# A recurrent cell and a routed layer on one core: the routed layers of the first two batches run one behind the other, with the second batch ranked and gathered in the same step

## Chip, core and metric

The kernel runs on one core of one Trainium2 chip. The metric is the device time of one execution in microseconds (us). Everything is float32, except the one-hot selection of the ranking, which is bfloat16.

## What is computed

An mLSTM cell runs over 4 batches, 8 heads, 768 positions and 40 features per head. Its output, seen as 320 features per position, goes through a "mixture of depths": per batch, the 128 positions with the highest score pass through a two-layer network and are added back.

```python
for t in range(S):                                  # mLSTM, per batch and head
    m_new = maximum(f_gate[t] + m, i_gate[t])
    f_stab, i_stab = exp(f_gate[t] + m - m_new), exp(i_gate[t] - m_new)
    C = f_stab * C + i_stab * outer(v[t], k[t])
    n = f_stab * n + i_stab * k[t]
    y[t] = sigmoid(o_gate[t]) * (C @ q[t]) / maximum(abs(n @ q[t]), 1.0)
x = y as (batch, position, 320)
scores = x @ w_gate                                 # routed layer, per batch
top = the 128 positions with the highest scores
out = x
out[top] = x[top] + sigmoid(scores[top]) * (relu(x[top] @ w1) @ w2)   # w1 320 x 1024, w2 1024 x 320
```

## The kernel before

The order of all instructions is written out by hand: each engine runs its own instructions in the order in which the Python functions issue them, and semaphores make it wait for operands and for buffers. The engines are TensorE (PE, matmuls and transposes), VectorE (DVE), ScalarE (ACT), GpSimd (POOL) and SyncE (SP, which issues the loads).

The cell is cut into 12 steps `n` of 256 positions, three per batch (batch 0 is steps 0 to 2, batch 3 is steps 9 to 11). The loop over `n` (line 658) computes step `n` and prepares step `n + 1`:

- `scores(n)` (L292) multiplies keys and queries on PE; `masked(n)` (L303) applies the causal mask on DVE and so gives the tile `P`.
- `turn(n + 1, "kT")` and `turn(n + 1, "qT")` (L223) transpose keys and queries on PE, and ACT copies them out of the matmul's accumulator memory (PSUM); `widen(n + 1)` (L214) is an ACT copy that the query transposes need.
- `weigh(n + 2)` (L239) multiplies values by gates on POOL; `update(n + 1)` (L259) forms the new state on PE and `states(n + 1)` (L271) adds it up on DVE.
- `read(n)` (L310) and `attend(n)` (L327) accumulate the step's output on PE; `divide(n)` (L336) normalizes it on DVE; `sigmoid(n)` (L247, four ACT instructions) and `output(n)` (L349, two POOL products) apply the output gate; `store(n)` (L357) issues two stores to DRAM from POOL's queue.
- `router(n)` (L364) computes the scores of the routed layer on DVE.

The routed layer of a batch `b` goes through this chain:

- `spread(b)` (L397): six PE transposes spread the 768 scores over all partitions, and ACT copies them out.
- `ranks(b)` (L422): DVE counts for three columns how many scores are greater (L415), ACT does so for the other three by signs (L420); `select(b)` (L467) builds the one-hot selection on DVE.
- `numbers(b)` (L510): six small PE matmuls give the positions, and `index(b)` (L473) turns them into indices with four small DVE instructions.
- `fetch(b)` (L517): POOL issues an indirect DMA that gathers the 128 rows from the stored output in DRAM.
- `fetched(b)` (L524): three PE transposes of the gathered rows, three ACT copies; `valued(b)` (L536): the gate of each row, on DVE and ACT.
- `layer1(b, f0)` (L545): half of the first layer, 12 matmuls and one ACT relu. With `b == 0` it works before the change on both halves of the tiles `xeT_t` and `hT_t`, 256 columns, which are batches 0 and 1 together. `layer2(b)` (L565): 8 matmuls per batch; `weighed(b)` (L575): ACT scales the result out of PSUM; `add(b)` (L584): POOL issues an indirect DMA that adds the rows to the output in DRAM.

PSUM is held by four pools: `ps_s`, `ps_u` and `ps_h` with one buffer each of two banks, and `ps_t` with two buffers of one bank each. Scores, `spread` and the second half of the first layer share `ps_s`; state updates and the first half of the first layer share `ps_u`; `read`/`attend` hold `ps_h` until `divide` has read it; transposes, gathered rows and `layer2` rotate through `ps_t`. So a tile is written only when the reader of its predecessor in that buffer has finished.

The chain of batch 0 stands before the change in steps 3 (`spread`), 4 (`ranks`, `select`, `numbers`) and 5 (`fetch`); that of batch 1 in steps 6 (`spread`) and 7 (`ranks`, `select`, `numbers`, `fetch`). Step 8 is written out in the function `layers` (L625): both batches are transposed there, their first layer runs in two halves over 256 columns, and the sigmoids, outputs, stores and scores of steps 6, 7 and 8, left out in steps 6 and 7, are done between. The third batch is spread, ranked and selected there too, with its numbers and its gather in step 9.

Of the kernel before, what the change touches and what calls it, by code (L numbers as in the profile page):

```python
# [9 lines left out]
FP = mybir.dt.float32  # L10
# [16 lines left out]
def _fast(ctx, tc, q, k, v, i_gate, f_gate, o_gate, w_gate, w1_in, w2_in, out):  # L27
# [6 lines left out]
    NS = S // 256  # L34
# [179 lines left out]
    def widen(n):  # L214

        ACT.copy(out=qw_t[n % 2][:, :, :, 0:D], in_=q_t[n % NB].rearrange("s h (t d) -> s t h d", t=2))  # L216
# [30 lines left out]
    def sigmoid(n):  # L247
        for r in range(2):
            for c in range(2):
                ACT.activation(out=so_t[n % 3][64 * c:64 * c + 64, r], in_=o_t[n % NO][64 * r:64 * r + 64, c], func=AF.Sigmoid)  # L250
# [76 lines left out]
    def attend(n):  # L327
        g = pending[n]
        for p in range(NP):
            for j in range(2):  # L330
                for c in range(2):
                    PE.matmul(g["pH"][64 * c:64 * c + 64, NP * j + p], g["P"][:, j, c, p, :], wv_t[n % 3][:, c, 2 * p + j],  # L332
                              start=(c, j) not in g["begun"], stop=True, skip_group_check=True)
                    g["begun"].add((c, j))

    def divide(n):  # L336
        b, s = divmod(n, NS)
        pH = pending[n]["pH"].rearrange("s h r x -> s r h x")
        den = work.tile([128, 2, H], FP, name="den")
        nq = pH[:, :, :, D]  # L340
        DVE.scalar_tensor_tensor(out=den, in0=nq, scalar=-1.0, in1=cols[s][:, 2:4, b * H:b * H + H], op0=OP.mult, op1=OP.max)
        DVE.scalar_tensor_tensor(out=den, in0=nq, scalar=LEAST * LEAST, in1=den, op0=OP.max, op1=OP.max)
        rec = work.tile([128, 2, H], FP, name="rec")
        DVE.reciprocal(out=rec, in_=den)
        y = work.tile([128, 2, H, D], FP, name="y", bufs=4)
        DVE.tensor_tensor(out=y, in0=pH[:, :, :, 0:D], in1=rec.unsqueeze(3).to_broadcast([128, 2, H, D]), op=OP.mult)
        pending[n]["y"] = y

    def output(n):  # L349
        b, s = divmod(n, NS)  # L350
        for r in range(2):
            x, o = x_t[b % 2][:, 2 * s + r, 0:DM], so_t[n % 3][:, r].rearrange("s h d -> s (h d)")
            order = "s (p j d) -> s j p d"
            POOL.tensor_tensor(out=x.rearrange(order, j=2, d=D), in0=pending[n]["y"][:, r].rearrange("s (j p) d -> s j p d", j=2),  # L354
                               in1=o.rearrange(order, j=2, d=D), op=OP.mult)

    def store(n):  # L357
        b, s = divmod(n, NS)
        for c in range(2):
            a = 256 * s + 128 * c  # L360
            (POOL if n < N - 1 else SP).dma_start(out=out[b, a:a + 128, :].rearrange("(r t) d -> t r d", t=64),  # L361
                          in_=x_t[b % 2][64 * c:64 * c + 64, 2 * s:2 * s + 2, 0:DM])
# [31 lines left out]
    def half(b):  # L394
        return slice(128 * (b % 2), 128 * (b % 2) + 128)
# [128 lines left out]
    def fetched(b, count=0):  # L524
        d, xe = dep[b], xe_t[b % 2]
        pX = ps_t.tile([128, 3, 128], FP, name="pX", tag="t")
        fill(pX[:, 0, :], count)
        for j in range(3):
            w = min(128, DM - 128 * j)
            PE.transpose(pX[0:w, j, :], xe[:, 128 * j:128 * j + w], ident)  # L530
        d["xeT"] = xeT_t[:, :, half(b)]
        ACT.copy(out=d["xeT"][:, 0:2], in_=pX[:, 0:2])
        for i in range(2):
            ACT.copy(out=d["xeT"][64 * i:64 * i + 64, 2], in_=pX[0:64, 2])

    def valued(b):  # L536
        d, xe = dep[b], xe_t[b % 2]
        scr = work.tile([128, DM], FP, name="scr", bufs=1)
        sg = mod.tile([128, 1], FP, name="sg")
        DVE.tensor_tensor_reduce(out=scr, in0=xe[:, 0:DM], in1=wg, scale=1.0, scalar=0.0, op0=OP.mult, op1=OP.add,  # L540
                                 accum_out=sg)
        d["g"] = mod.tile([128, 1], FP, name="g")
        ACT.activation(out=d["g"], in_=sg, func=AF.Sigmoid)

    def layer1(b, f0):  # L545

        d = dep[b]
        w = 256 if b == 0 else 128
        xeT, hT = (xeT_t, hT_t) if b == 0 else (xeT_t[:, :, half(b)], hT_t[:, :, half(b)])
        if b in (0, B - 1) and f0 > 0:  # L550
            ph = ps_s.tile([128, 2, 512], FP, name="ph", tag="s")
        else:
            ph = ps_u.tile([128, 2, 512], FP, name="pU")
        ph = ph[:, :, 0:2 * w].rearrange("s i (f e) -> s f i e", e=w)
        for f in range(4):
            for j in range(2):
                PE.matmul(ph[:, f // 2, f % 2, :], w1[:, j, (f0 + f) * 128:(f0 + f) * 128 + 128], xeT[:, j, :],  # L557
                          start=(f < 2 and j == 0), stop=False, skip_group_check=True)
        for f in range(4):
            o = slice(64 * (f % 2), 64 * (f % 2) + 64)  # L560
            PE.matmul(ph[:, f // 2, f % 2, :], w1c[o, (f0 + f) // 2, :], xeT[o, 2, :], start=False, stop=True,  # L561
                      skip_group_check=True)
        ACT.activation(out=hT[:, f0:f0 + 4, :].rearrange("s (f i) e -> s f i e", i=2), in_=ph, func=AF.Relu)
# [61 lines left out]
    def layers(n):  # L625

        fetched(0)
        read(n)
        fetched(1)
        attend(n)  # L630
        divide(n)
        valued(0)
        valued(1)
        for i in range(n - 2, n + 1):
            sigmoid(i)
            output(i)
            store(i)
            if i < n:
                layer1(0, 4 * (i - n + 2))
            router(i)  # L640
        weigh(n + 1)
        layer2(0)
        dep[2] = {"sb": spread(2, 0, 2 * NS, ps_h)}
        ranks(2)
        weighed(0)
        layer2(1)
        add(0)
        weighed(1)
        select(2)
        weigh(n + 2)  # L650
        turn(n + 1, "kT")
        widen(n + 1)
        update(n + 1)
        states(n + 1)
        turn(n + 1, "qT")
        add(1)

    for n in range(N):
        b, s = divmod(n, NS)
        more = n + 1 < N  # L660
        todo = queue.get(n, ())
        for act, i in zip(todo[0::2], todo[1::2]):
            act(*(() if i is None else (i,)))
        scores(n)
        masked(n)
        if n == 8:
            layers(n)
            continue
        if n == 0:
            update(0)  # L670
            states(0)
        if n in (3, 6, 11):
            router(n - 1)
        if n in (4, 7):
            ranks(n // 3 - 1)
            select(n // 3 - 1)
        if more:
            turn(n + 1, "kT", (0, 2, 6, 2, 2, 4)[n] if n < 6 else 0)
            widen(n + 1)
        if 0 < n and more:  # L680
            update(n + 1)
            if n != 9:
                states(n + 1)
            if n not in (3, 6, 7, 9):
                router(n - 1)
        if not more:
            sigmoid(n)
            gated(n)
            fill(ps_t.tile([128, 128], FP, name="pf", tag="t"), 2)
        read(n)  # L690
        if n == 9:
            numbers(2, ps_s.tile([128, 2, 512], FP, name="pi", tag="s")[:, 0, 0:3])
            states(n + 1)
        if n + 2 < N and n != 7:
            weigh(n + 2)
        if n == 5:
            fetch(0)
        if n == 0:
            update(1)
            states(1)  # L700
        if more:
            turn(n + 1, "qT")
            if n in (3, 6):
                dep[n // 3 - 1] = {"sb": spread(n // 3 - 1, 0, 2 * NS)}
            if n == 7:
                numbers(1, spare(n + 1)[:, 1, 0:3])
                fetch(1)
            if n not in (6, 7):
                sigmoid(n)
        else:  # L710
            fetched(b - 1, 2)
            dep[b] = {"sb4": spread(b, 0, 4)}
            layer1(b - 1, 0)
            valued(b - 1)
            ranks_first(b)
        attend(n)
        divide(n)
        if n == 4:
            numbers(0, spare(n + 1)[:, 1, 0:3])
        if n == 9:  # L720
            fetch(2)
        if more and n not in (6, 7):
            output(n)
            store(n)
        if n == 0:
            POOL.memset(k_t[3][:, :, :, D:DP], 0.0)
            tables()
        if n == 1:
            margins()
# [376 lines left out]
```

## Time and profile before

| what | value |
|---|---|
| time, median of 3 runs | 167.95 us (167.4 to 170.14) |
| the profiled execution: its own time | 168.06 us |
| its span, first to last instruction | 166.2 us |
| granted clock of TensorE, mean (1 is full speed) | 0.952 |
| PE busy | 147.9 us, 89% of the span |
| DVE busy | 94.2 us, 57% |
| ACT busy | 88.6 us, 53% |
| POOL busy | 84.3 us, 51% |
| HBM traffic | 143 GB/s over the span |

How to read the profile: a row of a timeline or of a group gives the start and the length in us, the engine, the line of the kernel, the operation, `out<-in` by tile names, the operands' shapes and how many instructions are merged (`x32`); in square brackets stands how long the engine sat idle before it and what ended that. A float32 matmul of the source shows as two records, so 16 matmuls are `x32`. The rows of the chain of waits give start, length and what it was, each step being what released the next. A row of the windows of one engine gives the stretch, its length, the busy time with the number of instructions, the granted clock, the busy share of the DMA engines and their GB/s. Under DMA, "to landing" is the time from a transfer's issue to its last byte.

### The profile page before, as it was taken

To read this page: it belongs to the slowest core of one execution; us is meant where nothing else is said; L and a number is where in the kernel's file an instruction comes from. 1 tells how busy PE (TensorE), PEld (TensorE's weight loads), DVE (VectorE), ACT (ScalarE), POOL (GpSimd) and SP (SyncE) were. 2 spreads that over 40 slices of the span, in tenths; PEclk is the share of its full clock that TensorE was granted. 3 is DMA by queue.
4 is the path that set the end of the run, shared out by engine and by line. 5 is a ranking of instruction groups with operands and counts; after the bars stand their busy time and mean duration, and the time that the engine had idled before them with its cause. 6 is when DMAs were issued, how large, how long until landed. Compare 5 with 4: busy or idle time off the path is not lost.

```text
span 166.2 us, 6581 instructions
## 1 busy us (share of the span) xinstructions
PE 147.9 (89%) x2816; PEld 127.7 (77%) x2816; DVE 94.2 (57%) x251; ACT 88.6 (53%) x177; POOL 84.3 (51%) x114
## 2 busy tenths in 40 slices
PE   7999899999989899994949999997999999999900
PEld 7889789897978898894838786766899898898600
DVE  6567466477689966898513322465496969511010
ACT  1577397556698545792011566593577859312000
POOL 7146379878582859920200476956775644122020
PEclk9999999999999999999675899999999999999985
DMA  4999899999979999999989999973313030330110
GB/s 89 196 161 191 146 175 204 185 222 183 224 154 237 173 209 187 201 351 185 300 181 172 187 236 238 187 153 43 43 28 93 7 83 0 79 43 6 43 51 2
DMA packets 91880, 24.31 MB, mean 146 GB/s; under 512 B 88097, under 2 KB 90466, under 8 KB 91842
## 3 DMA queue, kind: packets, MB, share of 16 engines
q1 hardware_dynamic: 89920, 18.75, 63.2%
q0 software_dynamic: 1728, 4.92, 11.4%
q8 instruction: 24, 0.39, 1.0%
q10 hardware_dynamic: 194, 0.13, 0.3%
q14 instruction: 14, 0.11, 0.2%
HBM read 19.20 MB, written 4.59 MB: 143 GB/s over the span
## 4 chain that ended last, share of the span: by engine, by line
PE 55%; DMA 12%; DVE 10%; ACT 7%; issue 7%; POOL 4%; SPq 0%; POOLq 0%; DVEq 0%; ACTq 0%
PE pt L232 9%; PE pH L332 7%; PE pU L557 6%; DMA xe<-out_dram,idx 6%; PE pU L267 6%; PE py L573 5%; PE pH L322 3%; PE pS L300 3%; DMA k<-in_k_dram 3%; PE warm L99 3%; DMA v<-in_v_dram 3%; POOL wv L244 2%; ACT sgn L420 2%; PE ph L557 2%; PE pU L561 2%
## 5 line engine op out<-in xcount | busy, mean ns | idle before, releaser
L244 POOL TENSOR_TENSOR wv<-v,cols 64x656 f32<-64x656 f32 x23 | 30.3, 1318 | 21.2 <-DMA v<-in_v_dram 7.5
L354 POOL TENSOR_TENSOR x<-y,so 128x320 f32<-128x320 f32 x24 | 21.4, 904 | 23.7 <-ACT so L250 15.1
L250 ACT ACTIVATE so<-o 64x320 f32<-64x320 f32 x48 | 22.5, 468 | 0.9
L236 ACT COPY qT<-pt 128x512 f32<-128x512 f32 x24 | 13.8, 634 | 16.0 <-PE pt L232 16.0
L369 DVE CUSTOM_DVE_ANT_0 scr<-x,wg 128x320 f32<-128x320 f32 x22 | 13.7, 623 | 14.1 <-POOL x L354 12.9
L234 ACT COPY kT<-pt 128x512 f32<-128x512 f32 x24 | 13.1, 586 | 12.0 <-PE pt L232 12.0
L332 PE MATMUL pH<-wv,P 128*64 128x82 f32 x384 | 18.4, 255 | 0.0
L573 PE MATMUL py<-w,hT 128*128 128x320 f32 x64 | 18.1, 436 | 0.0
L332 PEld LDWEIGHTS pH<-wv,P 128*64 128x64 f32 x384 | 16.3, 150 | 2.0 <-issue 1.6
L267 PE MATMUL pU<-wv,k 128*64 128x82 f32 x384 | 16.5, 237 | 1.0 <-issue 0.6
L267 PEld LDWEIGHTS pU<-wv,k 128*64 128x64 f32 x384 | 14.5, 137 | 3.0 <-issue 2.7
L300 PE MATMUL pS<-qT,kT 40*64 40x64 f32 x768 | 15.0, 226 | 1.6 <-ACT qT L236 1.1
L306 DVE TENSOR_TENSOR P<-pS,mask 128x1024 f32<-128x1024 f32 x12 | 14.6, 1218 | 2.4 <-PE pS L300 2.2
L279 DVE TENSOR_TENSOR C<-pU,C 128x164 f32<-128x164 f32 x40 | 13.1, 327 | 4.9 <-PE pU L267 3.8
L300 PEld LDWEIGHTS pS<-qT,kT 40*64 40x64 f32 x768 | 13.1, 140 | 3.2 <-ACT qT L236 1.5
L573 PEld LDWEIGHTS py<-w,hT 128*128 128x128 f32 x64 | 11.8, 190 | 4.8 <-issue 0.3
L361 POOL DMA_DIRECT2D out_dram<-x x22 | 13.9, 634 | 3.3 <-POOL x L354 3.3
L232 PE MATMUL pt<-ident,k 128*128 128x128 f32 x96 | 13.9, 282 | 0.8 <-DMA k<-in_k_dram 0.6
L322 PE MATMUL pH<-C,qT 40*64 40x41 f32 x704 | 13.7, 229 | 0.0
L232 PE MATMUL pt<-ident,qw 128*128 128x128 f32 x96 | 13.0, 279 | 0.6 <-ACT qw L216 0.5
L322 PEld LDWEIGHTS pH<-C,qT 40*64 40x64 f32 x704 | 12.4, 134 | 1.4 <-issue 0.5
L420 ACT ACTIVATE sgn<-sb,x 128x768 f32<-128x768 f32 (+2 forms) x16 | 12.8, 801 | 0.5
(141 smaller groups left out, 220.6 us busy)
## 6 DMA issues: line engine op xcount, KB each, us to landing
k<-in_k_dram SPq DMA_DIRECT2D x24, 160.0 KB, 4.8
q<-in_q_dram SPq DMA_DIRECT2D x12, 320.0 KB, 5.1
v<-in_v_dram SPq DMA_DIRECT2D x24, 160.0 KB, 4.5
o<-in_o_gate_dram SPq DMA_DIRECT2D x24, 160.0 KB, 4.6
out_dram<-x POOLq DMA_DIRECT2D x22, 160.0 KB, 3.9
w<-in_moe_w_dram SPq DMA_DIRECT2D x2, 640.0 KB
w<-in_moe_w_dram SPq DMA_DIRECT2D x2, 512.0 KB
out_dram<-x SPq DMA_DIRECT2D x2, 160.0 KB
```

The source lines that it names most:

```text
L232: PE.transpose(pt[:, p, :], src[:, c, 2 * p:2 * p + 2, :].rearrange("s j d -> s (j d)"), ident)
L244: (DVE if n == 0 and r else POOL).tensor_tensor(out=wv_t[n % 3][o, :, :, r], in0=v_t[n % NB][o], op=OP.mult, in1=cols[s][o, 0:2, b * H:b * ...
L250: ACT.activation(out=so_t[n % 3][64 * c:64 * c + 64, r], in_=o_t[n % NO][64 * r:64 * r + 64, c], func=AF.Sigmoid)
L267: PE.matmul(pU[64 * j:64 * j + 64, c, p], k_t[n % NB][:, c, 2 * p + j, :], wv_t[n % 3][:, c, 2 * p + j], start=True, stop=True)
L300: PE.matmul(pS[o, j, c, p, :], kT[e, p, t], qT[e, p, t], start=True, stop=True)
L306: DVE.tensor_tensor(out=P.rearrange(flat), in0=pending[n].pop("pS").rearrange(flat), op=OP.mult, in1=mask.unsqueeze(1).to_broadcast([128, ...
L322: PE.matmul(g["pH"][64 * c:64 * c + 64, NP * j + p, r], g["qT"][e, p, t], state[n, 2 * c + r][e, p, :], start=(c, j) not in g["begun"], st ...
L332: PE.matmul(g["pH"][64 * c:64 * c + 64, NP * j + p], g["P"][:, j, c, p, :], wv_t[n % 3][:, c, 2 * p + j], start=(c, j) not in g["begun"], ...
L354: POOL.tensor_tensor(out=x.rearrange(order, j=2, d=D), in0=pending[n]["y"][:, r].rearrange("s (j p) d -> s j p d", j=2), in1=o.rearrange(o ...
L361: (POOL if n < N - 1 else SP).dma_start(out=out[b, a:a + 128, :].rearrange("(r t) d -> t r d", t=64), in_=x_t[b % 2][64 * c:64 * c + 64, 2 ...
L420: ACT.activation(out=sgn[:, 0:w], in_=sb, func=AF.Sign, bias=own, scale=-1.0, accum_out=cnt)
L573: PE.matmul(d["py"], hT_t[:, f, half(b)], w2[:, f, :], start=(f == 0), stop=(f == NF - 1))
```

## The change

In step 8 the first layer of batch 0 runs alone over 128 columns (two halves, with `divide(8)` behind the second on DVE), then its second layer; behind them come the transposes of the gathered rows of batch 1 and its first layer, and later its second layer. Batch 1 is spread in step 7 instead of 6, behind the query transposes, and its `ranks`, `select`, `numbers` and `fetch` move from step 7 into step 8: the counts stand behind the mask of step 8, the numbers between the two halves of batch 0's first layer, and the gather behind the store of step 6 on POOL's queue. The numbers use a `ps_t` buffer there instead of a corner of the state's tile. The second half of the first layer uses `ps_s` for every batch but batch 2. The sigmoids, outputs and stores of steps 6, 7 and 8 keep their order but are spread between the new pieces; the routers of steps 6 and 7 stand behind `layer2(0)`, that of step 8 behind the first half of batch 1's first layer. `add(0)` stands directly behind `weigh(9)`, the key transposes of step 9 ahead of `spread(2)`, and `update(9)` behind `weigh(10)` and `select(2)` as before. The gather of batch 0 is issued in step 6, behind `weigh(8)`, instead of step 5.

```diff
@@ -545,9 +545,9 @@
     def layer1(b, f0):
 
         d = dep[b]
-        w = 256 if b == 0 else 128
-        xeT, hT = (xeT_t, hT_t) if b == 0 else (xeT_t[:, :, half(b)], hT_t[:, :, half(b)])
-        if b in (0, B - 1) and f0 > 0:
+        w = 128
+        xeT, hT = xeT_t[:, :, half(b)], hT_t[:, :, half(b)]
+        if b != 2 and f0 > 0:
             ph = ps_s.tile([128, 2, 512], FP, name="ph", tag="s")
         else:
             ph = ps_u.tile([128, 2, 512], FP, name="pU")
@@ -626,30 +626,43 @@
 
         fetched(0)
         read(n)
-        fetched(1)
+        ranks(1)
+        select(1)
         attend(n)
+        layer1(0, 0)
+        sigmoid(n - 2)
+        output(n - 2)
+        store(n - 2)
+        numbers(1, ps_t.tile([128, 3], FP, name="pi", tag="t"))
+        fetch(1)
+        layer1(0, 4)
         divide(n)
         valued(0)
+        sigmoid(n - 1)
+        output(n - 1)
+        store(n - 1)
+        layer2(0)
+        router(n - 2)
+        router(n - 1)
+        weighed(0)
+        sigmoid(n)
+        output(n)
+        store(n)
+        fetched(1)
         valued(1)
-        for i in range(n - 2, n + 1):
-            sigmoid(i)
-            output(i)
-            store(i)
-            if i < n:
-                layer1(0, 4 * (i - n + 2))
-            router(i)
+        layer1(1, 0)
+        router(n)
+        layer1(1, 4)
         weigh(n + 1)
-        layer2(0)
+        add(0)
+        turn(n + 1, "kT")
+        widen(n + 1)
         dep[2] = {"sb": spread(2, 0, 2 * NS, ps_h)}
         ranks(2)
-        weighed(0)
         layer2(1)
-        add(0)
         weighed(1)
         select(2)
         weigh(n + 2)
-        turn(n + 1, "kT")
-        widen(n + 1)
         update(n + 1)
         states(n + 1)
         turn(n + 1, "qT")
@@ -671,9 +684,9 @@
             states(0)
         if n in (3, 6, 11):
             router(n - 1)
-        if n in (4, 7):
-            ranks(n // 3 - 1)
-            select(n // 3 - 1)
+        if n == 4:
+            ranks(0)
+            select(0)
         if more:
             turn(n + 1, "kT", (0, 2, 6, 2, 2, 4)[n] if n < 6 else 0)
             widen(n + 1)
@@ -693,18 +706,15 @@
             states(n + 1)
         if n + 2 < N and n != 7:
             weigh(n + 2)
-        if n == 5:
+        if n == 6:
             fetch(0)
         if n == 0:
             update(1)
             states(1)
         if more:
             turn(n + 1, "qT")
-            if n in (3, 6):
-                dep[n // 3 - 1] = {"sb": spread(n // 3 - 1, 0, 2 * NS)}
-            if n == 7:
-                numbers(1, spare(n + 1)[:, 1, 0:3])
-                fetch(1)
+            if n in (3, 7):
+                dep[n // 4] = {"sb": spread(n // 4, 0, 2 * NS)}
             if n not in (6, 7):
                 sigmoid(n)
         else:
```

## The prediction

> **What bounds the kernel now.** I read the page first, then the chain of waits, then TensorE's windows and timeline around step 8. Batches are 0 to 3; step 8 is the last of batch 2. Times are us from the span's start.
>
> ```profile
> span 166.2 us, 6581 instructions
> PE 147.9 (89%) x2816; PEld 127.7 (77%) x2816; DVE 94.2 (57%) x251; ACT 88.6 (53%) x177; POOL 84.3 (51%) x114
> ```
>
> TensorE (PE) is busy 89% of the span, so an edit is worth what it gives PE: idle time taken away, or slow time.
>
> ```profile
> 73.22 0.94 DVE cmp L415 x2
> ...
> 76.38 0.96 DVE sel L469
> ...
> 78.36 0.31 PE pU L514 x6
> ...
> 80.03 6.28 DMA xe<-out_dram,idx
> ...
> 89.64 5.02 PE pU L557 x16
> ```
>
> The chain leaves PE in step 7: DVE ranks batch 1 and builds its selection, PE's six numbers matmuls wait for that, the second gather waits for them, and `attend` of step 8 stands behind the gather.
>
> ```profile
> 68.33 0.82 PE L405 MATMUL pB<-ident,x 128*128 128x128 f32 x6
> 69.08 1.36 PE L332 MATMUL pH<-wv,P 128*64 128x82 f32 x32
> ...
> 75.02 1.09 PE L232 MATMUL pt<-ident,qw 128*128 128x128 f32 x8
> 78.36 0.29 PE L514 MATMUL pU<-place,sel 128*128 128x3 bf16 x6 [2.25 <-DVE C L279]
> 78.58 2.37 PE L332 MATMUL pH<-wv,P 128*64 128x82 f32 x32
> 80.88 1.71 PE L300 MATMUL pS<-qT,kT 40*64 40x64 f32 x64
> ...
> 86.35 0.90 PE L530 MATMUL pX<-ident,xe 128*128 128x128 f32 x3 [2.21 <-DMA xe<-out_dram,idx]
> ```
>
> Two holes of 2.25 and 2.21 us. The same 32 matmuls of `attend` take 1.36 in step 6 and 2.37 in step 7; the windows of PE (busy time, then granted clock) say why:
>
> ```profile
> 75.39:78.80 3.41, 1.16 (x17) 0.99 1.00 178
> 78.80:82.21 3.41, 3.41 (x84) 0.51 0.99 272
> 82.21:85.63 3.42, 1.93 (x94) 0.99 1.12 292
> 85.63:89.04 3.41, 2.69 (x31) 0.50 0.69 117
> 89.04:92.45 3.41, 3.41 (x17) 0.51 1.21 194
> ```
>
> After a stretch of 3.41 us with 1.16 or 1.93 us of work the clock stands at half for the next; it stays there after 2.69 of work, and comes back only after a full stretch. So the holes cost 4.5 us of idleness and three stretches at half speed.
>
> **The change part by part.** Durations come from this execution: 166.2 of span and 1.9 around it are its 168.06; the median of the runs is 167.95, so the two are within 0.1%.
>
> *Steps 5 to 7.* The first gather's issue leaves step 5 for step 6, behind `weigh(8)`:
>
> ```profile
> 64.70 1.14 POOL L520 DMA_INDIRECT xe<-out_dram,idx  x1 [0.28 <-POOL wv L244]
> ...
> 69.16 2.66 POOL L244 TENSOR_TENSOR wv<-v,cols 64x656 f32<-64x656 f32 x2
> ...
> DMA to landing us min/median/max: 3.0/3.7/6.3
> ```
>
> On POOL it stood ahead of `output(5)`, so that, its store and `weigh(8)` come 1.1 earlier and the gather itself 6 later, at 70.7 (71.82 less 1.1). By the longest landing seen it is there at 77.0; it is needed at 78.5 (below). I cost it at nothing; uncovered it would cost as much as it is late. `spread(1)` leaves step 6: PE gains 0.75 (68.33 to 69.08), and pays it again in step 7. The three counts, the halving, the selection (4.1 of DVE, 73.22 to 77.34) and the numbers leave step 7, and the 2.25 hole with them. PE ends step 7's transposes at 75.35 (76.11 less 0.75), `spread(1)` at 76.1, `attend(7)` at full clock at 77.4 (before: 80.95), `scores(8)` at 78.5, the first gather's transposes at 78.9.
>
> ```profile
> 80.99 0.17 DVE L341 SCALAR_TENSOR_TENSOR den<-pH,cols 128x16 f32<-128x16 f32 x1 [1.69 <-PE pH L332]
> ...
> 81.69 0.82 DVE L346 TENSOR_TENSOR y<-pH,rec 128x640 f32<-128x640 f32 x1
> 82.66 1.23 DVE L306 TENSOR_TENSOR P<-pS,mask 128x1024 f32<-128x1024 f32 x1
> ```
>
> `divide(7)` takes 1.5 on DVE (80.99 to 82.51), so DVE ends it at 78.9 and masks step 8 by 80.1. `read(8)` fits under the mask; `attend(8)` runs from 80.1 to 81.4.
>
> ```profile
> 95.65 3.72 PE L557 MATMUL ph<-xeT,w 128*128 128x256 f32 x16
> 99.30 1.13 PE L561 MATMUL ph<-xeT,w1c 64*128 64x256 f32 x8
> 100.36 4.58 PE L573 MATMUL py<-w,hT 128*128 128x320 f32 x16
> ...
> 111.15 1.35 PE L267 MATMUL pU<-wv,k 128*64 128x82 f32 x32
> 114.44 1.16 PE L300 MATMUL pS<-qT,kT 40*64 40x64 f32 x64 [0.77 <-ACT qT L236]
> 136.67 2.05 PE L557 MATMUL pU<-xeT,w 128*128 128x128 f32 x16
> 138.65 0.72 PE L561 MATMUL pU<-xeT,w1c 64*128 64x128 f32 x8
> ```
>
> Before, the layers began behind it at 89.6 (the chain's last row): PE is 8.2 us ahead there.
>
> *The layers.* A half of the first layer over both batches takes 4.7 at full clock (95.65 to 100.36); over one batch 2.6 (the last rows, less their overlap). Four of 2.6 against two of 4.7 add 1.0 of PE. After `attend(8)` comes the first of them, to 84.0. DVE counts and selects from 80.1 to 84.3 (4.1 as above), so the numbers wait 0.3 and end at 84.6; the second half ends at 87.2 and `layer2(0)`, 4.5, at 91.7. Here the new wait stands: PE's next work is the second gather's transposes.
>
> ```profile
> 92.30 1.93 ACT L250 ACTIVATE so<-o 64x320 f32<-64x320 f32 x4
> 139.47 0.58 ACT L563 ACTIVATE hT<-pU 128x512 f32<-128x512 f32 x1
> 109.57 0.93 ACT L582 ACTIVATE yg<-py,g 128x320 f32<-128x320 f32 x2
> 87.29 0.37 ACT L532 COPY xeT<-pX 128x256 f32<-128x256 f32 x1 [3.40 <-PE pX L530]
> 93.33 2.10 POOL L354 TENSOR_TENSOR x<-y,so 128x320 f32<-128x320 f32 x2 [12.21 <-ACT so L250]
> 95.73 1.25 POOL L361 DMA_DIRECT2D out_dram<-x  x2 [0.30 <-POOL x L354]
> ...
> DMA to landing us min/median/max: 4.0/4.0/4.1
> ```
>
> POOL issues that gather behind `output(6)` and `store(6)`. From the start of the four sigmoids to the end of the store's issue it is 4.7 (92.30 to 96.98). ACT has the first half's relu at 84.6, so the gather is issued at 89.3. It lands between 3.0 and 6.3 later; I take 4.0, what the stores in this stretch of loads took: 93.3. But ACT, which must copy its transposes, has `weighed(0)` (0.46) and the sigmoids of step 8 (1.93) ahead, from 91.7 to 94.1. With the 0.37 of the first copy the layers of batch 1 start at 94.5, for any landing before 93.6.
>
> *From there to step 9* PE has two halves (5.2), the key transposes (1.0), `spread(2)` (0.7), `layer2(1)` (4.5), `update(9)` (1.3), query transposes (1.0) and 0.8 for the last copy: 14.5, so `scores(9)` would start at 109.0. Moving the key transposes ahead of `spread(2)` changes the order, not the sum; ACT's key copies now precede the signs of batch 2, which lie under `layer2(1)`; if they outlast it, `weighed(1)` holds a bank that the query transposes need. POOL's `weigh(9)` (2.66) stands behind the store of step 8, issued by 92.2 + 4.7 = 96.9, and is needed by `update(9)` at 105.9: no cost. SP's order is unchanged, but the weights are needed earlier, the last of them at 87.2 instead of 100.4:
>
> ```profile
> 77.64 1.25 SPq L619 DMA_DIRECT2D w<-in_moe_w_dram  x2
> ```
>
> If they take as long as the slowest gather, 6.3 from 78.9, they are there at 85.2. I cost this at nothing; the cover is 2 us.
>
> *The clock.* The hole from 91.7 to 94.5 holds 0.4 of work: 2.4 idle. A stretch with 1.5 us of idleness has put the next at half speed, one with 0.7 has not (the windows above). Most placements give one slow stretch (+1.7), some two (+2.9, since part of the first is idle), an even split perhaps none. I take one: `scores(9)` at 110.7, against 114.44. From there both kernels run the same work without a hole, so the gain is 3.7 to 3.8, and 168.06 becomes 164.3.
>
> A rule of the Trainium skill speaks for more: "TensorE: Matmul & The Clock Gate", section "HAM oscillation — how this bites in real kernels", has gaps of over about 3.4 us drop the clock. By it a hole of 2.4 would cost no clock; here the trace disagrees, since 2.25 did (the window from 75.39).
>
> **The rivals.**
>
> *The second gather lands late.* For it: 6.3 landed under load, and the store's packets are just ahead in POOL's queue. Against: the other two, 3.0 and 3.7. At 6.3 it lands at 95.6, the layers start at 96.4, 1.9 later, and the hole of 4.3 brings two slow stretches: 109.0 + 1.9 + 2.5 is 113.4, and the time 167.0; at 5.2 it is 165.9.
>
> *The clock stays full.* The hole is split so that neither stretch has 1.5 idle: 109.0, and 162.6. The Trainium skill's rule above gives the same time. For it: 0.7 was harmless; against: 2.25 in one stretch was not.
>
> *Slower: the gather queues behind the store.* If the 4.0 of the store and the 6.3 of the gather came one after the other, it lands at 99.6 and `scores(9)` starts at 100.4 + 14.5 + 2.5 = 117.4: 171.0. It decides from a landing 7.3 us after the issue (96.6), where the gain is gone. Against: the stores' 4.0 counts from their own issue, so they are partly done when the gather is issued. The Trainium skill ("DMA: Bandwidth & Descriptors", section "Two DMAs through the same engine are not ordered") has descriptors of one queue start in order but pipelined; by it the gather waits for the store's start, not its landing, and no run here shows that yet.
>
> *The change doesn't do what it says:* the hole of step 7 reappears ahead of the numbers in step 8, because DVE's counts end later than 84.3 (say by 2 us, as POOL and DVE slowed each other's work). Then everything behind comes 2 later: 166.3.
>
> **How the numbers follow.** One or two slow stretches: 0.55, at 164.3 (two: 165.5). Late gather: 0.17, 165.9 to 167.2. Full clock: 0.14, 162.6. Gather behind the store: 0.08, 167.5 to 173. Counts late: 0.06, 166.3. The range from 162.4 to 167.2 leaves out the slower rival and the tails, about 0.15. Two per cent, about what a measurement of this kernel can tell from no change, is 164.6 or 171.3 against the median. Faster by over 2%: the full clock (0.14), two thirds of the first case (0.36): 0.50. Slower by over 2%: half of the slower rival, 0.04. Within: 0.46.
>
> **What would show it.** Right: `attend(7)` at 1.3 to 1.4 us and no hole ahead of it; `attend(8)` ending 7 to 9 us earlier; one hole on PE of 2 to 3.5 us behind `layer2(0)`, with a slow stretch behind it; the gather issued about 89 and landed by 94; `scores(9)` near 110.7. Wrong: a gather landing over 5 us after its issue, a hole ahead of the numbers over 1 us, a wait for weights ahead of a layer, or a second hole between the layers of batch 1 and step 9.

## The result, and the profile after

| | before | after |
|---|---|---|
| time, median of 20 runs each | 168.48 us (167.03 to 172.72) | 167.05 us (166.01 to 171.63) |
| the profiled execution: its own time | 168.06 us | 167.68 us |
| its span | 166.2 us | 165.6 us |
| granted clock of TensorE, mean | 0.952 | 0.962 |
| `scores(9)` starts | 114.44 us | 113.84 us |

The ratio of the times is 0.9908, with a 95% interval of 0.9879 to 0.9938: the kernel is faster by about 0.9%, less than half of the 2.2% that was forecast (168.06 to 164.3). The time lies inside the forecast's range, at the place of one of its rivals, the late second gather (165.9 to 167.2). A profile shows one execution only: that of the changed kernel took 167.68 us, the longest of the 13 fast runs on which its ratio rests (mean 166.6), and that of the first experiment below took 166.35 us, 1.8% above the fastest run of its kernel, so a difference between two traces is good only to 1 or 2 us.

The head of the page of the changed kernel, and its row of the granted clock in 40 slices of 4.14 us:

```profile
span 165.6 us, 6677 instructions
PE 146.7 (89%) x2864; PEld 127.9 (77%) x2864; DVE 96.2 (58%) x251; ACT 88.9 (54%) x179; POOL 83.7 (51%) x114
...
PEclk9999999999999999999999957999999999999975
```

One dip is left there, from 95 to 103 us (the last two slices are the end of the kernel, where the row of before dips too). TensorE's timeline of the changed kernel, from the end of step 7 to the scores of step 9:

```profile
64.72 1.26 PE L232 MATMUL pt<-ident,k 128*128 128x128 f32 x8 [0.89 <-DMA k<-in_k_dram]
...
75.14 1.09 PE L232 MATMUL pt<-ident,qw 128*128 128x128 f32 x8
76.07 0.82 PE L405 MATMUL pB<-ident,x 128*128 128x128 f32 x6
76.82 1.36 PE L332 MATMUL pH<-wv,P 128*64 128x82 f32 x32
...
79.91 0.80 PE L322 MATMUL pH<-C,qT 40*64 40x41 f32 x41 [0.16 <-DVE y L346]
81.05 0.56 PE L322 MATMUL pH<-C,qT 40*64 40x41 f32 x23 [0.34 <-issue]
81.53 1.36 PE L332 MATMUL pH<-wv,P 128*64 128x82 f32 x32
82.82 2.05 PE L557 MATMUL pU<-xeT,w 128*128 128x128 f32 x16
84.81 0.72 PE L561 MATMUL pU<-xeT,w1c 64*128 64x128 f32 x8
85.45 0.31 PE L514 MATMUL pi<-place,sel 128*128 128x3 bf16 x6
85.62 2.03 PE L557 MATMUL ph<-xeT,w 128*128 128x128 f32 x16
...
88.23 4.57 PE L573 MATMUL py<-w,hT 128*128 128x320 f32 x16
96.17 0.88 PE L530 MATMUL pX<-ident,xe 128*128 128x128 f32 x3 [3.36 <-DMA xe<-out_dram,idx]
97.50 3.78 PE L557 MATMUL pU<-xeT,w 128*128 128x128 f32 x16 [0.46 <-ACT xeT L532]
...
102.08 2.05 PE L557 MATMUL ph<-xeT,w 128*128 128x128 f32 x16
...
113.84 1.16 PE L300 MATMUL pS<-qT,kT 40*64 40x64 f32 x64 [0.77 <-ACT qT L236]
```

Both holes of steps 7 and 8 are gone: `attend(7)` (the first x32 of L332) follows `spread(1)` without a wait and takes 1.36 instead of 2.37, and the numbers (L514) wait for nothing. The first layer of batch 0 starts at 82.82, where the layers started at 89.64 before: 6.8 us ahead. But from there to `scores(9)` it is 31.0 us, against 24.8 before, so 6.2 of the 6.8 are given back. About 3.8 are the two new idle times in the rows (3.36 and 0.46), 1.0 the four halves over 128 columns in place of two over 256, 0.5 the transposes of batch 1 that stood ahead of the layers before, and 0.9 the clock: 2.3 us lost to it here (0.88 for the transposes against 0.55 at full speed, 3.78 and 0.94 for the first half against 2.05 and 0.72) against some 1.4 before, where half speed reached into the layers until 92.45.

The chain of waits of the changed kernel shows through what the new hole goes:

```profile
85.59 0.47 issue
86.06 0.46 ACT so L250
...
88.07 0.96 POOL x L354
89.03 0.29 issue
89.32 0.45 POOL out_dram L361
90.01 0.86 issue
90.87 5.16 DMA xe<-out_dram,idx
96.03 0.14 issue
96.17 0.89 PE pX L530 x3
97.08 0.38 ACT xeT L532
```

The sigmoids and products of step 6 and the issue of its store, then the gather's 5.16, then the copy. ACT's own queue (start and length of each row) had been done 1.8 us before the copy:

```profile
92.90 0.53 ACT L582 ACTIVATE yg<-py,g 128x320 f32<-128x320 f32 x1 [1.89 <-PE py L573]
93.32 1.92 ACT L250 ACTIVATE so<-o 64x320 f32<-64x320 f32 x4
97.08 0.37 ACT L532 COPY xeT<-pX 128x256 f32<-128x256 f32 x1 [1.83 <-PE pX L530]
```

The windows of PE in the changed kernel (stretch, length, busy time, granted clock, DMA share, GB/s):

```profile
88.06:91.47 3.41, 3.41 (x18) 1.00 1.23 188
91.47:94.88 3.41, 1.33 (x5) 1.00 1.15 280
94.88:98.29 3.41, 1.66 (x6) 0.50 1.20 242
98.29:101.71 3.42, 3.42 (x19) 0.50 1.19 272
101.71:105.12 3.41, 3.41 (x36) 1.00 0.86 141
```

The hole straddles two stretches: behind the 2.1 us of idleness in the first (from 91.47) the second already runs at half speed, and so does the one behind it. The Trainium skill's rule that gaps of over about 3.4 us drop the clock ("TensorE: Matmul & The Clock Gate", section "HAM oscillation — how this bites in real kernels") is neither borne out nor refuted by this hole, which is 3.36 us long; the hole of 2.56 us in the first experiment below speaks against it, since the clock stood at 0.50 in the stretch behind it (97.48 to 100.90).

### The profile page after: what moved, and what is told of

The parts are those of the page before. It is cut to its first block, busy times and chain, and to the rows that moved or that the text cites. A ratio compares the mean times of both kernels' runs of the same rounds, so it can differ in the third digit from the quotient of the medians.

```text
span 165.6 us, 6677 instructions
## 1 busy us (share of the span) xinstructions
PE 146.7 (89%) x2864; PEld 127.9 (77%) x2864; DVE 96.2 (58%) x251; ACT 88.9 (54%) x179; POOL 83.7 (51%) x114
## 4 chain that ended last, share of the span: by engine, by line
PE 52%; DMA 18%; POOL 9%; issue 7%; ACT 5%; DVE 4%; SPq 0%; POOLq 0%; DVEq 0%
PE pt L232 8%; PE pU L267 7%; PE pU L557 7%; DMA k<-in_k_dram 7%; DMA v<-in_v_dram 6%; PE py L573 5%; DMA xe<-out_dram,idx 5%; PE pH L322 5%; PE pH L332 5%; POOL wv L244 4%; PE warm L99 3%; PE pS L300 3%; POOL x L354 3%; PE pU L561 2%; ACT qT L236 2%
## 5 line engine op out<-in xcount | busy, mean ns | idle before, releaser
L354 POOL TENSOR_TENSOR x<-y,so 128x320 f32<-128x320 f32 x24 | 20.7, 878 | 24.7 <-ACT so L250 15.0
L369 DVE CUSTOM_DVE_ANT_0 scr<-x,wg 128x320 f32<-128x320 f32 x22 | 15.4, 698 | 6.2 <-POOL x L354 4.3
L279 DVE TENSOR_TENSOR C<-pU,C 128x164 f32<-128x164 f32 x40 | 13.1, 328 | 6.6 <-PE pU L267 5.5
L415 DVE TENSOR_SCALAR_CACHE_REDUCE cmp<-sb,x 128x768 f32<-128x768 f32 (+2 forms) x14 | 12.0, 858 | 8.1 <-ACT sb L409 7.7
L332 PE MATMUL pH<-wv,P 128*64 128x82 f32 x384 | 16.3, 237 | 0.0
L332 PEld LDWEIGHTS pH<-wv,P 128*64 128x64 f32 x384 | 14.4, 136 | 1.9 <-issue 1.2
L300 PE MATMUL pS<-qT,kT 40*64 40x64 f32 x768 | 14.2, 221 | 1.1 <-ACT qT L236 1.1
L300 PEld LDWEIGHTS pS<-qT,kT 40*64 40x64 f32 x768 | 12.5, 134 | 2.5 <-ACT qT L236 1.5
L232 PEld LDWEIGHTS pt<-ident,k 128*128 128x128 f32 x96 | 10.4, 140 | 3.8 <-PE pt L232 1.2
```

Source lines behind the costliest of these rows:

```text
L232: PE.transpose(pt[:, p, :], src[:, c, 2 * p:2 * p + 2, :].rearrange("s j d -> s (j d)"), ident)
L300: PE.matmul(pS[o, j, c, p, :], kT[e, p, t], qT[e, p, t], start=True, stop=True)
L369: DVE.tensor_tensor_reduce(out=scr, in0=x[:, r, 0:DM], in1=wg, scale=1.0, scalar=0.0, op0=OP.mult, op1=OP.add, accum_out=x[:, r, DM:DM + 1])
```

## The experiments

The theory after the result (A): the gather of batch 1 is the late end, by its place behind the store and by its 5.16 of landing. Its rivals: B, ACT's sigmoids of step 8 stand right behind it as the next late end, so that an earlier gather alone brings little; Q, the store's packets on the same queue make the landing long; C, the clock is the price and not the hole; and, for the change as a whole, that the split of the layers rather than the moved ranking brings the gain. All ratios are to the kernel before; the change's own is 0.9908.

### The order of gather and sigmoids

**The gather ahead of output and store of step 6**

```diff
         sigmoid(n - 2)
-        output(n - 2)
-        store(n - 2)
         numbers(1, ps_t.tile([128, 3], FP, name="pi", tag="t"))
         fetch(1)
+        output(n - 2)
+        store(n - 2)
```

> The second gather is issued ahead of the output and the store of step 6 on POOL instead of behind them; nothing else changes. Theory A (the hole ahead of the layers of batch 1 is the gather alone: issued at 90.9, landed 5.2 later): issued at about 86.9 and landed by 92.1, the hole (3.4 us in the changed kernel) closes nearly, no slow clock, scores of step 9 near 108.5, ratio to the kernel before about 0.96. Theory B (ACT, with the scaling of batch 0 and the sigmoids of step 8 ahead of the copies, is right behind the gather): the gather lands by 92.1, but the copies wait for ACT until 95.3; the layers start at 95.7 instead of 97.5, scores of step 9 at 111 to 112, ratio 0.978 to 0.983. Theory Q (the packets of the store held up the gather on POOL's queue): the time from issue to landing falls from 5.2 to under 4.

Measured: 0.9762 (0.9696 to 0.9828). PE's timeline and then ACT's in this kernel:

```profile
93.50 0.49 PE L530 MATMUL pX<-ident,xe 128*128 128x128 f32 x3
96.55 2.96 PE L557 MATMUL pU<-xeT,w 128*128 128x128 f32 x16 [2.56 <-ACT xeT L532]
```

```profile
94.19 1.92 ACT L250 ACTIVATE so<-o 64x320 f32<-64x320 f32 x4
96.13 0.37 ACT L532 COPY xeT<-pX 128x256 f32<-128x256 f32 x1
```

The gather is issued at 87.48 and has landed at 91.9; the transposes no longer wait for it. Now the copy stands behind the sigmoids of step 8 with no gap, and makes a hole of 2.56 in its turn. (So it does in the version with fillers below: the sigmoids end at 95.81, the copy starts at 95.83.) A and B both hold: two waits stand one behind the other. Q asked for a landing under 4 us; it was 4.4.

**The sigmoids, output and store of step 8 behind the copies**

```diff
         weighed(0)
+        fetched(1)
         sigmoid(n)
         output(n)
         store(n)
-        fetched(1)
```

> The sigmoids, output and store of step 8 stand behind the transposes and copies of the second gather; the gather itself is issued as in the changed kernel. Theory A: nothing gained, the gather lands at 96 as before and ACT had been free since 95.2: ratio 0.988 to 0.994, the hole 3.4 us. Theory B as predicted (ACT is what ends last): the layers of batch 1 start up to 2 us earlier, ratio about 0.98.

Measured: 0.9992 (0.9953 to 1.0032). The gather is issued at 90.84 as in the changed kernel and the hole is 3.03. Taken alone, the second wait is worth nothing, since the first ends later; the time is even 0.8% above the change's. The trace cannot explain that: its execution, at 166.53 us, is the fastest of this kernel's 12.

**Both**

> Both edits: the gather ahead of the output of step 6, and the sigmoids of step 8 behind the copies. Theory A alone: the same as with the first edit. Theory B: only with both does the hole close; layers of batch 1 start at about 93.5, no stretch at half speed behind them, scores of step 9 near 108.5, ratio 0.96 to 0.967.

Measured: 0.9623 (0.9561 to 0.9685), some 3% better than the change and better than either edit alone. PE's timeline and windows in this kernel:

```profile
87.39 4.57 PE L573 MATMUL py<-w,hT 128*128 128x320 f32 x16
91.80 0.49 PE L530 MATMUL pX<-ident,xe 128*128 128x128 f32 x3
92.90 2.05 PE L557 MATMUL pU<-xeT,w 128*128 128x128 f32 x16 [0.61 <-ACT xeT L532]
...
107.30 1.16 PE L300 MATMUL pS<-qT,kT 40*64 40x64 f32 x64 [0.78 <-ACT qT L236]
```

```profile
88.06:91.47 3.41, 3.41 (x14) 1.00 1.36 193
91.47:94.88 3.41, 2.80 (x21) 1.00 1.10 274
94.88:98.29 3.41, 3.41 (x34) 1.00 1.03 210
```

A hole of 0.61 is left, 0.6 us idle in a stretch does not touch the clock, and `scores(9)` starts at 107.30: 6.5 ahead of the changed kernel. (0.8 of that lies ahead of the first layer: no stall in `read(8)` and a key load in time. The two ratios are only 4.8 us apart; the two profiled executions are the shortest of this kernel's and the longest on which the change's ratio rests.)

**The rest of the hole covered**: as before, with the copies between the sixth and the seventh matmul of `layer2(0)`.

```diff
-        layer2(0)
+        layer2(0, 0, 6)
+        fetched(1)
+        layer2(0, 6, 8)
```

> Both edits that closed the hole (ratio 0.962), and the transposes of the second gather stand ahead of the last two of the eight matmuls of batch 0's second layer, so that their copies lie under these. Theory A and B with the gather landed by 90: the 0.6 us of waiting for the copies goes, ratio 0.957 to 0.960. If the gather lands after 91, PE waits for it there and nothing is gained: 0.962 to 0.966.

Measured: 0.9635 (0.957 to 0.97). The wait of 0.61 is gone in the trace, but `scores(9)` starts at 107.64 and the time is that of the version without it: nothing to be told apart at this size.

### How the time follows the gather

**The gather behind output and store of step 7**

```diff
         numbers(1, ps_t.tile([128, 3], FP, name="pi", tag="t"))
-        fetch(1)
...
         sigmoid(n - 1)
         output(n - 1)
         store(n - 1)
+        fetch(1)
```

> The second gather is issued behind the output and store of step 7 as well, 3.3 us later than in the changed kernel (about 94.2). Theory A: the hole grows by as much, scores of step 9 move by 3 us or a little more, ratio 1.008 to 1.014. Theory B (ACT ends last): a hidden part of the delay, ratio under 1.003.

Measured: 1.0145 (1.0067 to 1.0223). Issued 3.65 later (94.52), landed 4.3 later still, a hole of 5.64 behind `layer2(0)`, `scores(9)` at 116.75, 2.9 later than in the changed kernel, for a landing 2.8 later (98.8 against 96.0). In the traces the scores so follow the gather one to one, which A asks for; the two ratios are 4.0 us apart, with an interval of 1.3 us to either side.

**The gather between output and store of step 6**

```diff
         output(n - 2)
-        store(n - 2)
         numbers(1, ps_t.tile([128, 3], FP, name="pi", tag="t"))
         fetch(1)
+        store(n - 2)
```

> The second gather is issued between the output and the store of step 6: 1.5 us earlier than in the changed kernel (about 89.3), with no store's packets ahead of it. Theory Q (the store ahead on POOL's queue made the landing long): issue to landing under 4.5, where kernels with the store ahead showed 4.8 to 5.9; landed by 93.5, ACT sets the hole, ratio 0.975 to 0.980. Rival (the general load of transfers sets it): 5 or more, landed after 94, ratio 0.980 to 0.986.

Measured: 0.9791 (0.9739 to 0.9843). Issued at 89.69, landed 4.7 later. PE's rows show both ends nearly even, the gather first, then ACT:

```profile
94.51 0.52 PE L530 MATMUL pX<-ident,xe 128*128 128x128 f32 x3 [1.20 <-DMA xe<-out_dram,idx]
96.20 3.56 PE L557 MATMUL pU<-xeT,w 128*128 128x128 f32 x16 [1.18 <-ACT xeT L532]
```

The store alone, moved past the gather, is worth 1.2%, and nearly all that the first experiment gained: the gather is issued 1.2 earlier and lands 0.5 faster. The landing of 4.7 lies between what Q asked for (under 4.5) and what its rival did (5 or more).

*The landing over all runs.* Each of the 14 traces holds four gathers of 128 rows. The table has their time from issue to landing, and beside it what all DMA engines of the core moved meanwhile:

| gathers | moved meanwhile, GB/s | landed after, us |
|---|---|---|
| batches 2 and 3 (28) | 41 to 63 | 3.0 or 3.1, once 4.4 |
| batch 0 in step 5, as before the change (2) | 163 and 181 | 3.7 and 4.1 |
| batch 1 in step 8, no store right ahead (5) | 155 to 208 | 3.3 to 4.7 |
| batch 1 in step 8, store of step 6 right ahead (the change and four experiments) | 249 to 265 | 4.8 to 5.9 |
| batch 1 in step 8, behind the stores of steps 6 and 7 (1) | 262 | 4.3 |
| batch 1 in step 7, no store in the 10 us ahead (before, and the split alone, twice) | 279 to 288 | 6.3 to 6.6 |
| batch 0 in step 6 (12) | 238 to 282 | 5.4 to 6.8 |

Among the gathers of step 8 those behind the store took 1.2 us longer (mean 5.2 against 4.0), as Q would have it. But the longest landings had no store right ahead, and the one behind two stores took 4.3. What sorts the rows is the load: up to 4.7 below 210 GB/s, 4.3 to 6.8 above 235. So Q is not supported, and its rival, the general load of transfers, fits far better; no run changed the load alone, so that it sets the landing is not shown.

That store and gather take their times one after the other (the forecast's slower rival) is excluded: the forecast had 10.3 us for it. The Trainium skill's "DMA: Bandwidth & Descriptors", section "Two DMAs through the same engine are not ordered", has them start in order and overlap; the 5.16 agrees with that.

### The clock

**12 filler matmuls, which nobody reads, in the hole ahead of the transposes** (`fetched(1, 12)` in the changed kernel)

> Twelve matmuls of 128 columns on a constant (3.0 us of PE) fill the hole ahead of the transposes of the second gather; nothing else changes, their result is overwritten. Theory C (two stretches at half speed cost 2.0 us of the changed kernel's 2.6 us longer way through the first half of batch 1's layer): the gather still lands at 96, the clock stays full, scores of step 9 at 111.8, ratio about 0.979. If the clock costs nothing of note, or drops all the same: ratio 0.988 to 0.994.

Measured: 0.9895 (0.983 to 0.996), no different from the change. PE's rows in this kernel:

```profile
97.86 2.05 PE L557 MATMUL pU<-xeT,w 128*128 128x128 f32 x16 [0.46 <-ACT xeT L532]
...
112.25 1.16 PE L300 MATMUL pS<-qT,kT 40*64 40x64 f32 x64 [0.77 <-ACT qT L236]
```

The clock stays full and the way from the first layer of batch 1 to `scores(9)` is 14.4 against 16.3: 2.0 us are the clock's price there. But the gather landed 5.9 after its issue.

**The same in the version with the gather first** (`fetched(1, 8)`)

> The gather ahead of the output of step 6, as in the first experiment (ratio 0.976, ACT sets the hole, PE idle for 2.6 us), and eight matmuls on a constant (2.0 us) in that hole ahead of the transposes; the fill ends before ACT is free, so it delays nothing. Theory C (the half-speed stretch behind the hole costs 1.3 to 1.7 us): the clock stays full, the first half of batch 1's layer takes 2.6 instead of 4.1, ratio 0.965 to 0.970. If the clock costs nothing of note in timed runs: 0.974 to 0.978.

Measured: 0.9832 (0.9773 to 0.989), no better than without the filler (0.9762; the intervals overlap, and the medians of all six runs are 166.1 with it and 166.0 without). In the trace the first half of the layer takes 2.6 and `scores(9)` starts 1.85 earlier, 1.6 of it behind the start of the layer. So one pair of executions shows the clock's price at 2.0 us and one at 1.6, and the timed runs show no gain either time.

The mean granted clock of each run is known and says part of why. A stretch of 3.41 us at half speed takes 0.010 off the mean of a kernel of 165 us. The change's 13 runs stand at 0.971 in the mean (the profiled one at 0.962), the four with twelve fillers at 0.982: by that the fillers won back about one stretch, and not the two of the profiled execution. It is an estimate only, since half speed at the kernel's end, where PE idles, takes off as much and more, and not the same in each run: 0.019 in the trace with twelve fillers, 0.009 in that with the sigmoids behind the copies. C is therefore at work, probably for less than 2 us in the mean run; its size stays open.

### The parts of the change alone

**Only the layers split; spread, ranking, numbers and gather of batch 1 stay in steps 6 and 7**

```diff
         read(n)
-        ranks(1)
-        select(1)
         attend(n)
...
-        numbers(1, ps_t.tile([128, 3], FP, name="pi", tag="t"))
-        fetch(1)
...
-            if n in (3, 7):
-                dep[n // 4] = {"sb": spread(n // 4, 0, 2 * NS)}
+            if n in (3, 6):
+                dep[n // 3 - 1] = {"sb": spread(n // 3 - 1, 0, 2 * NS)}
+            if n == 7:
+                numbers(1, spare(n + 1)[:, 1, 0:3])
+                fetch(1)
```

(and `ranks`, `select` in step 7 again)

> One part of the change alone: the layers of batches 0 and 1 run one behind the other in step 8, but batch 1 is spread in step 6 and ranked, numbered and gathered in step 7 as before the change. Theory A (the gain of the change is given back in the wait for the second gather, which it issues 11 us later than before): the hole of 2.3 us and one slow stretch stay in step 7, but the gather, issued at 80, has landed long before PE asks for it at about 90, so no hole stands ahead of the layers of batch 1 unless ACT's sigmoids of step 8 make one of 2 to 3 us; scores of step 9 at 110 to 112, ratio 0.97 to 0.985, faster than the whole change. Rival: what the change gains comes from taking the ranking out of step 7, and the split alone gives nothing or loses (1.0 us more of PE): ratio 0.995 to 1.005.

Measured: 1.0084 (1.0038 to 1.0129), slower than before, and a miss. PE's timeline in this kernel:

```profile
78.58 0.30 PE L514 MATMUL pU<-place,sel 128*128 128x3 bf16 x6 [1.99 <-DVE C L279]
78.81 2.46 PE L332 MATMUL pH<-wv,P 128*64 128x82 f32 x32
...
101.03 2.83 PE L557 MATMUL pU<-xeT,w 128*128 128x128 f32 x16 [2.56 <-ACT xeT L532]
...
116.97 1.16 PE L300 MATMUL pS<-qT,kT 40*64 40x64 f32 x64 [0.77 <-ACT qT L236]
```

The hole of step 7 (1.99) and the slow `attend(7)` (2.46) are there as before. The gather lands long before it is needed, and still a hole of 2.56 opens behind `layer2(0)`: ACT's sigmoids, as in the first experiment. The windows of PE behind the hole of step 7:

```profile
78.21:81.62 3.41, 3.04 (x54) 0.50 0.96 200
81.62:85.04 3.42, 3.42 (x104) 0.50 1.05 349
85.04:88.45 3.41, 3.41 (x66) 0.50 1.01 175
```

The clock stays at half for three stretches, though PE is busy in all of the second. With one more behind the second hole this trace has four slow stretches, before had three. That, and the 1.0 us of the narrower halves, is about what `scores(9)` lost against before (116.97 against 114.44). The split alone costs; with the split in place, the ranking's new place is worth the difference to the change, 1.8%. The new place without the split was not run.

**The same with the sigmoids of step 8 behind the copies**

> The split alone (ranking in step 7, ratio 1.008; its gather had landed long before, and PE stood idle 2.6 us behind the transposes), with the sigmoids of step 8 behind the copies. Theory B (there too ACT alone made the hole): the hole and its slow stretch go, 3 to 4 us, ratio 0.985 to 0.992. Rival (the loss of the split lies elsewhere, in the narrower matmuls or in step 7): under 1 us, ratio above 1.002. Either way what then separates it from 0.962 is the ranking's hole and slow clock in step 7.

Measured: 1.0132 (1.0067 to 1.0197), another miss. The hole behind `layer2(0)` fell from 2.56 to 0.61, as it should. But PE shows a stall inside `read(8)` that waits for nothing which the profile shows:

```profile
86.33 1.08 PE L322 MATMUL pH<-C,qT 40*64 40x41 f32 x29 [2.33 <-issue]
```

In this trace `scores(9)` still starts 0.9 earlier than without the edit (116.11 against 116.97). From the start of the layers it gains 2.4 us (26.4 against 28.8), but the layers start 1.5 later (89.72 against 88.21), behind this stall and three smaller ones in steps 6 and 7 (0.78, 0.39 and 0.19). The hole of 2.00 ahead of the numbers cost no clock here. It fell evenly over two stretches, which were busy for 2.31 and 2.33 of their 3.41 us, and the clock stayed at 1.00. Why these stalls came, and why the time is not lower at all, stays open.

**The first gather issued in step 5 again**

> One small part undone: the first gather is issued in step 5, ahead of the output of step 5 on POOL, as before the change. As costed in the prediction (nothing, its landing is covered either way, and the 1.1 us that POOL gains in step 5 lie under loads): ratio 0.987 to 0.995. Rival (POOL's earlier output and weighing in steps 5 and 6 are worth something): up to 1 us slower, ratio 0.997.

Measured: 0.9834 (0.9762 to 0.9905), an interval that overlaps the change's. The first gather's new place is worth nothing that these runs can tell from zero; if anything, it costs a little.

**Key transposes of step 9 behind the second layer again**

```diff
-        turn(n + 1, "kT")
-        widen(n + 1)
         dep[2] = {"sb": spread(2, 0, 2 * NS, ps_h)}
...
         weigh(n + 2)
+        turn(n + 1, "kT")
+        widen(n + 1)
```

> The other small part undone: the key transposes of step 9 and the widening stand behind the second layer of batch 1 and the ranking of batch 2, as before the change. As costed (the order changes, not the sum): ratio 0.988 to 0.996. Rival (the key copies wait behind the signs on ACT and hold the query transposes): 0.5 to 1 us slower than the changed kernel, ratio 0.994 to 0.998.

Measured: 0.9974 (0.9925 to 1.0024), some 0.6% above the change, with intervals that overlap a little. The transposes ahead of `spread(2)` may be worth half a per cent, as the rival has it; the runs do not show it clearly, and this profile does not show where it would lie: `scores(9)` starts at 113.27, no later than in the changed kernel.

## Why the prediction was partly wrong

- **Steps 5 to 7: right.** The hole and the slow stretch behind it went, `spread(1)` moved without a wait, `attend(7)` took 1.36. The hole of before was a little more than the ranking, though: its releaser in the row is `C L279`, the sums of the state, which stood behind the selection on DVE (77.26 to 78.31) and whose tile the numbers shared; at their new place the numbers have a tile of their own. The first gather was covered (issued at 71.81, landed at 77.4, needed at 79.2), and the step 5 experiment bears that out; the 1.1 us on POOL did not come, since `weigh(7)` waited until 62.94 for its load.
- **"PE is 8.2 us ahead": 6.8.** PE came to `attend(7)` 0.7 late (a wait of 0.89 for the key load of step 7, at 64.72), and `read(8)` did not fit under the mask: it began only when `divide(7)` had released its buffer (the row with `y L346`), and stalled 0.34, so that it ended at 81.6, the mask at 80.9. `attend(8)` so ended at 82.9 instead of 81.4.
- **"The gather is issued at 89.3 … I take 4.0 …: 93.3": the step that failed.** From the start of the sigmoids to the gather's issue it took 4.8 (86.06 to 90.87) against 4.7, so the length was right; it started 1.5 late with PE. The landing was 5.16 against 4.0. The gather landed at 96.0, 2.7 later than predicted, and became the late end instead of ACT. The layers of batch 1 started at 97.5, 3.0 later than 94.5, which is all but 0.1 of the 3.1 by which `scores(9)` missed 110.7. The mechanism, a new wait behind `layer2(0)`, was named; which of its two ends comes last was wrong, and so was its size. The 1.5 was in no row of before. The 4.0 was a choice: between a bound of 6.3 and a bound of 3.0, the stores' median, for another kind of transfer. The gather of batch 1 itself had taken the 6.3, at 279 GB/s, against 3.7 at 163 and 3.0 at 60 for the others; in the changed kernel it flew at 255.
- **"But ACT … for any landing before 93.6": right, and hidden.** The experiment with the gather first uncovered exactly this wait, at 96.1 instead of 94.1.
- **The clock: right in sum.** From the start of batch 1's layers to `scores(9)` 16.2 was predicted with one slow stretch, and 16.3 came. But the trace has two slow stretches, of which the first was in part idle, so the agreement is in part luck. Two readings behind the forecast were too simple. That a stretch "with 0.7 has not" put the next at half speed rests on the stretch from 85.63, which was itself at half speed and was followed by another; that so little is harmless was shown only by the experiment with both edits (0.6 idle). And the clock did not come back after each full stretch, as the split alone shows.
- **The weights of the first layer, asked for earlier, the numbers, and `weigh(9)`:** no wait for any of them shows in the rows; costed at nothing, rightly. The slower rival (gather after the whole store) and the late counts did not come.

## What to carry to other kernels

When a gather moves into the step that uses it, list what stands ahead of it on its own queue and what stands ahead of its consumer's copies on theirs, and move both: work with no early due time (an output product, a store, sigmoids of another step) goes behind. Two waits in series must be moved together: here one alone brought 1.5%, the other alone nothing, both 3%. And where the sum's likeliest case rests on a landing time between far bounds, read beside each landing what else was moved meanwhile, and take the one under the same load, not the median of another transfer.

## What the runs showed of the hardware

The same gather of 128 rows landed 3.0 to 6.8 us after its issue: 3.0 or 3.1 in 27 of 28 cases when the core moved 41 to 63 GB/s meanwhile, 4.3 to 6.8 when it moved over 235. Idle times well under a stretch of 3.41 us halved TensorE's clock for one or two stretches behind: 1.5 us idle in a stretch did (1.93 busy, before), 1.1 did not (2.31 and 2.33 busy, the split with the sigmoids behind). At half speed one fully busy stretch brought the clock back in several traces, and did not in the split alone. And runs of small float32 matmuls stalled now and then for 0.2 to 2.3 us with no releaser in the trace; what makes these stalls the runs do not show.
